# A kernel whose issue order comes from a planner: a finer model of DMA transfers, and another load order

## The chip, the cores and the metric

The kernel runs on one core of one Trainium2 chip. The metric is device time in microseconds (us) of one execution; a timed run takes about 2 us more than the span of its profile. Where two kernels are compared, the ratio is worked out from the fast runs of both in the same rounds on the same chip, so it is not quite the ratio of the medians that are quoted beside it. Runs are in the fast state but for one of e2, of e7 and of e13 and two of the four of e8; the medians are of all runs, the ratios leave the slow ones out.

Names in the profile: PE is TensorE (matmul), PEld its weight loads, DVE VectorE, ACT ScalarE, POOL GpSimd, SP the sync engine. SPq and ACTq are the queues from which SP and ACT issue DMAs.

## The reference, cut to what matters

```python
# q, k, v: (4, 8, 768, 64) float32; w_in (512, 2048), w_out (2048, 512)
scores = (q @ k.T) / 8;  keep = (pos_k < 4) | (0 <= pos_q - pos_k < 128)    # 4 sinks + window
a = softmax(where(keep, scores, -1e9)) @ v
x = a.transpose(0, 2, 1, 3).reshape(3072, 512)
h = x @ w_in
out = (h * sigmoid(1.702 * h)) @ w_out                                     # float32
```

## The kernel before

The 3072 rows are worked in 12 blocks of 256 rows (k = 0 to 11), in float16 on chip. For one block, in order:

1. `load(k)`: q, k and v (512 KB each) are loaded from the SP queue; POOL casts them.
2. `turn(k)`, from block 3 on: four transposing DMAs bring q and k into the layout that the scores need ("the q/k transposes").
3. Scores and sink scores on PE, exp on ACT, mask on DVE, then attention times v on PE and the normalization on DVE (`xb`).
4. `xturn`, from block 3 on: one transposing DMA of the normalized rows (`xT <- xb`, "the x transpose").
5. `mm1` (64 matmuls with `w_in`), tanh, `mm2` (32 matmuls with `w_out`), and the output stores.

The blocks overlap. No order is written by hand: each piece is an `Op` with a planned duration, and a list scheduler (`Plan.run`) simulates the engines at build time. The instructions are emitted in the order of the planned start times. The numbers in the plan thus reach the chip only through what the planner chooses with them: which instruction stands ahead of which in each engine's queue, and also which engine makes a cast, which buffer is taken, and how many filler matmuls (matmuls on zeros in PE's idle time at the start) are put in.

```python
HOP = {("PE", "ACT"): 60, ...}
class Plan:
    def run(self, warm=None, ...):
        ...
            free[e] = s + dur                        # the issuing engine is free again
            if isinstance(lat, tuple):               # a DMA
                dma_free = max(s + 2000, dma_free) + lat[0]
                o.end = dma_free + 300               # its data have landed
            ...
        order.sort(key=lambda x: (x[0], x[1]))       # by planned start
        return [(fn, e) for _, _, fn, e in order]

def turn(k):                                         # q/k transposes of block k, k >= 3
    ...
    casts = [o_cqk[k, p, e] for p in range(NP) for e in range(2)]
    for j in range(2):
        for i in range(2):
            def f(i=i, j=j): nc.sync.dma_start_transpose(...)
            o_t.append(op("SP", 1400, (800,), f, casts + war, prio=..., kind="turn"))

def back(k, p):                                      # attention x v, normalization
    ...
    o_t = op("SP", 2300, (1600,), lambda: nc.sync.dma_start_transpose(xT..., Xb...),
             [o_xT["n", k, q_] for q_ in range(NP)] + ..., kind="xturn")

LOADS = ["a0", "w0", "a1", "w1", "w2", "w3", "a2", "w4", "w5", "w6", "w7"]   # a: q,k,v of a block; w: weights
```

All transposes are issued from SP. The Trainium skill, "DMA: Bandwidth & Descriptors" (section "Silent corruption: two transposing streams in flight at once"), says that transposes issued from SP and from ACT can corrupt each other when both are in flight.

The softmax here doesn't subtract the row's maximum and nothing guards it: scores larger than these inputs give would overflow.

## Time and profile before

| | before |
|---|---|
| median of the first three runs | 232.47 us (230.57 to 232.59) |
| span of the profiled run | 232.3 us |
| PE busy | 94% |
| PE waits from 17 us on, plus time lost to a half-rate clock | 7.05 + 1.71 us |

The last row is summed from slices of 1 us: PE's idle part of each slice, and (1 - granted clock) times its busy part; the tail after the last matmul is left out.

The list of waits of PE in the kernel before (engine, its line, what it waited for: total us, times, longest us):

```profile
PE bank L542 <- DMA w<-qk: 2.5, 1, 2.5
PE bank L664 <- DMA xT<-xb: 1.3, 2, 0.9
...
PE bank L507 <- DMA w<-qk: 0.6, 1, 0.6
```

L542 are the scores, `w<-qk` the q/k transposes (they write into the freed weight buffers), L664 is `mm1`, L507 the sink scores. Busy time of each engine by stretch, kernel before; the columns are PE, PEld, DVE, ACT, POOL busy us (instructions), then the granted TensorE clock, the DMA share and GB/s:

```profile
60.00:64.00 4.00, 1.52 (x16) 0.74 (x15) 0.72 (x2) 1.34 (x3) 2.31 (x6) 1.00 0.74 138
64.00:68.00 4.00, 4.00 (x26) 2.05 (x25) 1.73 (x5) 1.81 (x6) 0.00 (x0) 0.57 0.68 99
...
100.00:120.00 20.00, 20.00 (x178) 13.44 (x175) 11.43 (x25) 11.26 (x22) 7.12 (x12) 1.00 0.96 205
120.00:140.00 20.00, 20.00 (x204) 13.90 (x204) 11.44 (x23) 13.65 (x28) 8.13 (x15) 1.00 0.86 169
140.00:160.00 20.00, 20.00 (x199) 13.68 (x197) 12.02 (x26) 12.30 (x24) 5.88 (x12) 1.00 0.92 163
```

There is one hole of 2.48 us at 60 to 63 us, followed by about 3.4 us at half clock (1.71 us lost); from 100 us on PE is busy all the time.

### The profile page before, as it was taken

Reading aid. Unit: us, or ns where it says so; the run is one execution under the profiler, and the core shown is the slowest. Engines: PE = TensorE matmul, PEld = TensorE weight load, DVE = VectorE, ACT = ScalarE, POOL = GpSimd, SP = SyncE. Lnnn points to the kernel's source line nnn. Section 1 sums busy time; section 2 is a strip of 40 time slices with the busy share of each in tenths; the row PEclk is TensorE's granted clock in tenths of the full one; section 3 lists DMA queues with packets and bytes.
Section 4 is the critical chain, followed back from the end, with each engine's and each line's share of the span. In section 5 each row is a group of like instructions: output and inputs, shape, how many; then the busy total and the mean of one; then the engine's idle time right before and its main releaser. Section 6 shows DMA issues by size and latency. Waiting matters only on the chain.

```text
span 232.3 us, 5342 instructions
## 1 busy us (share of the span) xinstructions
PE 218.6 (94%) x2108; PEld 150.1 (65%) x2108; DVE 127.2 (55%) x279; ACT 131.0 (56%) x258; POOL 81.1 (35%) x141
## 2 busy tenths in 40 slices
PE   8987998999599899999999999999999999999992
PEld 8764885656345576766667666766766766766640
DVE  3667977624256476466646646655645655644310
ACT  1758658243357646746656756755666676544320
POOL 6567786568704417243052262340430000000000
PEclk9999999999979999999999999999999999999999
DMA  6999999979969999698897967997974222221223
GB/s 179 335 266 395 312 324 316 324 199 252 115 97 297 157 227 219 126 294 105 200 232 130 258 128 120 261 118 150 277 121 76 48 45 48 45 55 38 45 55 80
DMA packets 74871, 41.06 MB, mean 177 GB/s; under 512 B 30688, under 2 KB 67680, under 8 KB 74848
## 3 DMA queue, kind: packets, MB, share of 16 engines
q1 hardware_dynamic: 73008, 39.73, 75.2%
q10 hardware_dynamic: 1840, 1.02, 1.5%
q8 instruction: 16, 0.26, 0.5%
q14 instruction: 7, 0.06, 0.1%
HBM read 27.36 MB, written 6.29 MB: 145 GB/s over the span
## 4 chain that ended last, share of the span: by engine, by line
PE 64%; DMA 22%; SPq 9%; POOL 2%; issue 1%; DVE 1%; ACTq 0%; ACT 0%; POOLq 0%
PE bank L692 28%; PE bank L664 27%; DMA xT<-xb 5%; DMA v<-in_v_dram 5%; DMA w<-in_moe_w_in_dram 5%; PE bank L597 4%; DMA w<-in_moe_w_out_dram 4%; SPq L446 4%; PE bank L542 3%; DMA qk<-in_k_dram 2%; SPq L371 2%; SPq L317 2%; DMA w<-qk 1%; PE bank L507 1%; POOL v L262 1%
## 5 line engine op out<-in xcount | busy, mean ns | idle before, releaser
L664 PE MATMUL bank<-xT,w_in 128*128 128x256 f16 x768 | 101.8, 273 | 1.9 <-DMA xT<-xb 1.3
L692 PE MATMUL bank<-w_out,gT 128*128 128x512 f16 x384 | 100.7, 382 | 0.7 <-POOL w_out L262 0.7
L678 DVE SCALAR_TENSOR_TENSOR gT<-th,bank 128x512 f16<-128x512 f16 x96 | 65.6, 684 | 53.2 <-ACT th L676 52.6
L664 PEld LDWEIGHTS <-w_in 128*128 128x128 f16 x768 | 72.4, 98 | 25.6 <-issue 3.7
L676 ACT ACTIVATE th<-bank 128x512 f16<-128x512 f32 x96 | 57.6, 602 | 51.7 <-PE bank L664 49.6
L560 ACT ACTIVATE at<-bank 128x512 f16<-128x512 f32 (+1 forms) x96 | 50.3, 572 | 18.6 <-PE bank L542 18.5
L692 PEld LDWEIGHTS <-gT 128*128 128x128 f16 x384 | 35.8, 98 | 24.9 <-issue 2.4
L262 POOL CAST qk<-qk 128x512 f16<-128x512 f32 x42 | 24.6, 612 | 67.1 <-DMA qk<-in_q_dram 48.4
L567 DVE TENSOR_TENSOR at<-at,bank 128x1024 f16<-128x1024 f16 (+1 forms) x48 | 30.5, 636 | 21.3 <-ACT at L560 21.1
L262 POOL CAST v<-v 64x512 f16<-64x512 f32 (+1 forms) x48 | 28.5, 593 | 10.0 <-DMA v<-in_v_dram 7.9
L597 PE MATMUL bank<-v,at 128*128 128x65 f16 x352 | 21.9, 195 | 1.0 <-DVE at L567 0.7
L597 PEld LDWEIGHTS <-at 128*128 128x128 f16 x352 | 17.8, 98 | 6.2 <-DVE at L567 2.3
L710 ACT ACTIVATE osb<-bank 128x512 f32<-128x512 f32 (+1 forms) x24 | 14.2, 590 | 13.2 <-PE bank L692 12.5
L515 ACT ACTIVATE ats<-bank 128x256 f16<-128x256 f32 x32 | 12.8, 400 | 7.2 <-PE bank L507 7.1
L615 DVE RECIPROCAL rcp<-bank 128x4 f32<-128x4 f32 x48 | 8.6, 180 | 12.6 <-PE bank L597 12.2
L617 DVE TENSOR_TENSOR xb<-bank,rcp 128x256 f16<-128x256 f32 x36 | 15.0, 420 | 0.6
L597 PE MATMUL bank<-vs,ats 128*128 128x65 f16 x128 | 15.2, 193 | 0.0
L597 PEld LDWEIGHTS <-ats 128*128 128x128 f16 x128 | 12.0, 97 | 1.8 <-issue 0.2
L542 PE MATMUL bank<-w 64*128 64x128 f16 (+1 forms) x168 | 10.3, 246 | 2.5 <-DMA w<-qk 2.5
L542 PEld LDWEIGHTS <-w 64*128 64x128 f16 x192 | 6.3, 96 | 8.0 <-issue 7.4
L758 PE MATMUL bank<-zero 128*128 128x128 f16 x109 | 10.2, 260 | 1.0 <-DVE zero L275 1.0
L262 POOL CAST w_out<-w 128x1024 f16<-128x1024 f32 x8 | 8.1, 1042 | 4.7 <-DMA w<-in_moe_w_out_dram 4.7
(40 smaller groups left out, 87.9 us busy)
## 6 DMA issues: line engine op xcount, KB each, us to landing
out_dram<-osb SPq DMA_DIRECT2D x47, 128.0 KB, 2.5
qk<-in_q_dram SPq DMA_DIRECT2D x11, 512.0 KB, 4.4
qk<-in_k_dram SPq DMA_DIRECT2D x11, 512.0 KB, 5.6
v<-in_v_dram SPq DMA_DIRECT2D x11, 512.0 KB, 7.1
w<-in_moe_w_in_dram SPq DMA_DIRECT2D x4, 1024.0 KB, 9.1
w<-in_moe_w_out_dram SPq DMA_DIRECT2D x4, 1024.0 KB, 9.6
w<-qk SPq DMA_TRANSPOSE x36, 2.9
qk<-in_q_dram SPq DMA_DIRECT2D x4, 128.0 KB, 4.0
```

The source lines that it names most:

```text
L262: {"POOL": nc.gpsimd.tensor_copy, "DVE": nc.vector.tensor_copy, "ACT": nc.scalar.copy}[e](out=out, in_=in_)
L515: o_se[k, p] = op("ACT", TB / 1.2 + 50, TB / 1.2 + 170, lambda: nc.scalar.activation(out=As, in_=f32(o_k)[:, 0:TB], func=AF.Exp, scale=scale),
L542: nc.tensor.matmul(f32(o_s, 2 * n + i)[:, c : c + w], src[d, j], Q[d].rearrange("d j s -> d (j s)")[:, q0 : q0 + w], start=True, stop=True,)
L560: nc.scalar.activation(out=A[:, i, 0:W], in_=f32(o_s, 2 * n + i)[:, 0:W], func=AF.Exp, scale=scale)
L567: nc.vector.tensor_tensor(out=A[:, :, 0:W], in0=A[:, :, 0:W], in1=mask[:, c0 : c0 + W].unsqueeze(1).to_broadcast((P, 2, W)), op=ALU.mult,)
L597: nc.tensor.matmul(avp()[:, j, i], a_, v_, start=(n == 0), stop=(n == len(mms) - 1))
L617: o_n = op("DVE", 300, 425, lambda: nc.vector.tensor_tensor(out=X, in0=avp()[:, :, :, 0:D], in1=rc.to_broadcast((P, 2, 2, D)), op=ALU.mult ...
L664: nc.tensor.matmul(f32(holder[0])[:, bass.ts(e, TB)], w_in16[:, c, bass.ts(Fi, P)], X[:, c] if k < KX else X2[:, :, c], start=(c == 0), st ...
L676: o_t = op("ACT", 477, 600, lambda first=first: nc.scalar.activation(out=th[first.places[0]], in_=f32(first), func=AF.Tanh, scale=0.851), ...
L678: o_g[k, s] = op("DVE", 565, 690, lambda first=first, s=s: nc.vector.scalar_tensor_tensor(out=g[:, 2 * s : 2 * s + 2].rearrange("p a t -> ...
L692: nc.tensor.matmul(f32(holder[0]), g[:, Fi, bass.ts(j, P)], w_out16[:, Fi], start=(Fi == 0), stop=(Fi == NF - 1),)
L710: nc.scalar.mul(O[:, c], f32(holder[0])[:, c], 0.5)
```

## The change

The planner gets a finer model of transfers: space for descriptors (the single orders of which a transfer consists) in each issuing queue's ring, eight completion slots ("lanes": a DMA waits until an earlier one on its slot has landed), a shorter delay before the first byte, a longer one until the data have landed, and new issue times of transposes. The second block's q, k and v (`a1`) are loaded ahead of all weights, and block 0's q and k are split into three DMAs each, not four; the two halves of its v change queues. No arithmetic changes. The diff is cut to what matters.

```diff
+RING, LANES = 163, 8
...
+            if isinstance(o.engs[e][1], tuple) and len(landed) >= LANES:
+                s = max(s, landed[-LANES])
...
             if isinstance(lat, tuple):
-                dma_free = max(s + 2000, dma_free) + lat[0]
-                o.end = dma_free + 300
+                ns, nd = lat
+                t = s + dur
+                while sum(n * min(1.0, (b - t) / max(b - a, 1.0)) for a, b, n in ring[e] if b > t) + nd > RING:
+                    t += 25
+                free[e] = t
+                begin = max(s + 1300, dma_free)
+                dma_free = begin + ns
+                ring[e].append((begin, dma_free, nd))
+                o.end = dma_free + 900
+                landed.append(o.end)
...
-    LOADS = ["a0", "w0", "a1", "w1", "w2", "w3", "a2", "w4", "w5", "w6", "w7"]
+    LOADS = OPT.get("LOADS") or ["a0", "a1", "w0", "w1", "w2", "w3", "a2", "w4", "w5", "w6", "w7"]
...
-                o = op("SP", 450, (1790,), f, war, prio=prio + e / 2, kind="load")
+                o = op("SP", 450, (1720, 64), f, war, prio=prio + e / 2, kind="load")
...
-                o_t.append(op("SP", 1400, (800,), f, casts + war, prio=base - 9 * h8, kind="turn"))
+                o_t.append(op("SP", 1310, (1000, 16), f, casts + war, prio=base - 9 * h8, kind="turn"))
...
-                o_t = op("SP", 2300, (1600,), lambda: nc.sync.dma_start_transpose(
+                o_t = op("SP", 1400, (1600, 16), lambda: nc.sync.dma_start_transpose(
```

In the list below X is the x transpose of blocks 3, 4, 5, ..., `t` are pieces of q/k transposes (those of block k+2 come near X of block k), L is a block's loads:

```
before: t1x4 t0x4 L X t1x4 L X t0x4 L X    t1x4    L X    t0x4    L t1   X t1x3    L t0 X   t0x3 L t1 X t1x3 X X
after:  t1x4 t0x4 L X L t1x4 X t0x4 L t1 X t1x3 L t0 X t0x3 L t1x2 t1 X t1 L t0x3 t0 X L t1x3 t1 X X X
```

In the changed kernel one or more pieces of block k+2's transposes stand ahead of the x transposes of blocks 5 to 9. In the kernel before this is so for blocks 7 to 9 only.

More of the change, by code (lines that the diff above doesn't have):

```diff
@@ L79, in run @@
         dma_free = 0.0
+        ring, landed = {e: [] for e in ENGINES}, []
         order = []
@@ L275 @@
     o_zero = op("DVE", 100, 200, lambda: nc.vector.memset(zero, 0.0), prio=NEVER, kind="const")
-    o_ident = op("ACT", 420, (300,), lambda: nc.scalar.dma_start(const, const_d.ap()), prio=NEVER + 2.6, kind="load")
+    o_ident = op("ACT", 480, (300, 8), lambda: nc.scalar.dma_start(const, const_d.ap()), prio=NEVER + 2.6, kind="load")
     def ones():
@@ L301 @@
                  [o_zero], prio=NEVER + 8, kind="const")
+    OPT = globals().get("OPT", {})
     CAST_W = ["POOL ACT"] + ["POOL"] * 7
@@ L305 @@
     CAST_V = ["POOL ACT", "POOL"] + ["POOL"] * (NK - 2)
+    CAST_W, CAST_QK, CAST_V = OPT.get("W", CAST_W), OPT.get("QK", CAST_QK), OPT.get("V", CAST_V)
     o_win, o_wout = {}, {}
@@ L316, in weights @@
             src = moe_w_out[bass.ts(j - 4, 512), :].rearrange("(c p) f -> p c f", p=P)
-        o_l = op("SP", 450, (3000,), lambda: nc.sync.dma_start(dst, src), war, prio=at, kind="w")
+        o_l = op("SP", 400, (2880, 32), lambda: nc.sync.dma_start(dst, src), war, prio=at, kind="w")
         loads.append(o_l)
@@ L327, in weights @@
             (o_win if j < 4 else o_wout)[2 * (j % 4) + n] = o
-    L = 17300.0
-    LOADS = ["a0", "w0", "a1", "w1", "w2", "w3", "a2", "w4", "w5", "w6", "w7"]
+    L = OPT.get('L',17300.0)
+    LOADS = OPT.get("LOADS") or ["a0", "a1", "w0", "w1", "w2", "w3", "a2", "w4", "w5", "w6", "w7"]
     def load_at(x):
@@ L351, in load, with f @@
         if k == 0:
-            for p in range(NP):
+            for n, (p0, p1) in enumerate(((0, 1), (1, 2), (2, 4))):
                 for e, (eng, dma, src) in enumerate((("SP", nc.sync, q), ("ACT", nc.scalar, k_ap))):
-                    def f(p=p, e=e, dma=dma, src=src):
+                    def f(p0=p0, p1=p1, e=e, dma=dma, src=src):
                         dma.dma_start(
-                            dst[:, e, 2 * p : 2 * p + 2],
-                            src[b, 2 * p : 2 * p + 2, t0 : t0 + TB].rearrange("h (p i) d -> p h i d", i=2),
-                        )
-                    lq[p, e] = op(eng, 500, (450,), f, war, prio=NEVER + 2.5 + p / 8, kind="load")
+                            dst[:, e, 2 * p0 : 2 * p1],
+                            src[b, 2 * p0 : 2 * p1, t0 : t0 + TB].rearrange("h (p i) d -> p h i d", i=2),
+                        )
+                    o = op(eng, 500, (600 * (p1 - p0), 16 * (p1 - p0)), f, war, prio=NEVER + 2.5 + n / 8, kind="load")
+                    for p in range(p0, p1):
+                        lq[p, e] = o
         else:
@@ L373, in load @@
         if k == 0:
-            o_lv = [op("ACT", 500, (900,), lv(nc.scalar, slice(0, 4)), war, prio=NEVER + 2.7, kind="load"),
-                    op("SP", 500, (900,), lv(nc.sync, slice(4, 8)), war, prio=NEVER + 2.95, kind="load")]
-            loads.append(o_lv[1])
+            o_lv = [op("SP", 500, (900, 32), lv(nc.sync, slice(0, 4)), war, prio=NEVER + 2.7, kind="load"),
+                    op("ACT", 500, (900, 32), lv(nc.scalar, slice(4, 8)), war, prio=NEVER + 2.95, kind="load")]
+            loads.extend(o_lv)
         else:
-            o_lv = [op("SP", 450, (1790,), lv(nc.sync, slice(0, 8)), war, prio=prio + 0.6, kind="load")]
+            o_lv = [op("SP", 450, (1720, 64), lv(nc.sync, slice(0, 8)), war, prio=prio + 0.6, kind="load")]
             loads.append(o_lv[0])
@@ L726, in f @@
                     )
-                o_d = op(eng, 500, (400,), f, o_c, prio=prio, kind="out")
+                o_d = op(eng, 590, (420, 4), f, o_c, prio=prio, kind="out")
                 uses("osb", oi, o_d)
```

## The prediction

> **What bounds the kernel now.** Median 232.47 us; the profiled span is 232.3 us with one state of clock (0.991). I see three stages.
> 1. 0 to about 47 us: loads. The table of engine busy time by stretch shows the DMA share at 0.94 to 1.2 in nearly every 2 us from 2 to 46 us (about 390 GB/s while weights load, 260 to 300 while q, k, v blocks load). PE, in the timeline, runs 109 filler matmuls up to 15 us; from about 21 us on it is nearly full.
> 2. 60 to 70 us: a hole. PE waits 2.48 us (60.4 to 62.9) for the four transposing DMAs of block 3, the longest PE wait in the list of waits. Its granted clock is then 0.5 from 64 to about 67.6 us (slices of 1 us), which costs another 1.75 us; then 0.57 us more for block 4's transposes. Together about 4.8 us.
> 3. 72 us to the end: PE is busy all the time in the 50 us stretches, but for 0.94 and 0.37 us before the first matmuls on transposed x. Tail after the last matmul: about 4 us.
>
> The Trainium skill, "TensorE: Matmul & The Clock Gate" (Part 1), says that the gate halves the clock after an idle window of 3.4 us; the trace agrees with the length of the penalty (3.6 us at 0.5), though here 2.5 us of idleness was enough.
>
> **What the change does.** No arithmetic is added or removed; only orders, the split of block 0's q and k loads (8 DMAs to 6), and filler matmuls (109 to 137; 52 to 56 before the first transpose, 0.105 us each cold).
> - Block 1 (1.5 MB) is loaded before w0 (1 MB). Before, w0's cast started at 13.5 us and block 1's q, k, v casts at 15.5, 17.1, 18.9 us. At the rates above block 1 comes about 3 us earlier and w0 about 5 us later; w1 to w7 land when they did, since bytes are the same. Attention 1 runs earlier while weights arrive; the first 16 mm1 matmuls (1.75 us) move behind it. By 37 us PE must again wait for w_out, so most of the lead is eaten. Net: 0.5 to 1.5 us.
> - Block 3's four transposes are issued ahead of the two output stores that kept the queue 52.57 to 55.1 us (2.53 us). Their casts ended at 52.26 us, so they can start 2.5 us earlier, but behind block 4's loads in the same rings. PE comes to these scores after 8 fewer mm1 matmuls (0.87 us), so part of the wait stays: I expect 0.5 to 1.5 us, short enough not to drop the clock. Gain 2.5 to 3.5 us.
> - Block 4's transposes now follow three pairs of stores (1.17 us each), so a wait of 0.5 to 1.5 us may stand before its sink scores. Loss up to 1 us.
> - Steady state: same matmuls, PE bound, no change.
>
> Sum: 1.0 + 3.0 - 0.5 = about 3.5 us. Predicted 228.8 us, 80% range 225.8 to 231.5. Faster by over 2%: 0.33; within 2%: 0.62; slower: 0.05.
>
> **What would show it.** Block 1's first cast near 12.5 us; PE's wait for block 3's transposes under 1.5 us and no slice below clock 0.9 near 64 us; block 4's first score at 66 to 69 us (71.5 before); PE 100% busy from 100 to 200 us as before.
>
> **What would make it wrong.** If the transposes land behind block 4's loads as late as before (62.8 us), the hole stays or grows, the clock drops again and the gain is only about 1 us. If both holes close and attention 1 fills PE from 16 us, 225 us is possible. If fillers or the weight cast in ScalarE's order hold up the first blocks, the head gets slower.

Two figures in it are off: the slices of 1 us add up to 3.4 us at half clock, not 3.6, and the changed kernel runs 123 fillers, not 137.

## More of the kernel before

The SP queue of the kernel before around the x transpose of block 5, and POOL's casts of block 7 at that time (start us, us, engine, line, operation, count, and in brackets the idle time before it):

```profile
100.67 1.14 SPq L724 DMA_DIRECT2D out_dram<-osb  x2
102.91 2.08 SPq L624 DMA_TRANSPOSE xT<-xb  x1
105.09 5.38 SPq L446 DMA_TRANSPOSE w<-qk  x4
```

```profile
100.69 1.17 POOL L262 CAST qk<-qk 128x512 f16<-128x512 f32 x2 [6.13 <-DMA qk<-in_q_dram]
102.34 1.17 POOL L262 CAST qk<-qk 128x512 f16<-128x512 f32 x2 [0.48 <-DMA qk<-in_k_dram]
```

The x transpose of block 5 goes first; the four transposes of block 7, whose casts end at 103.51 us, follow.

## The result, and the profile after

The changed kernel took 239.56 us (median of 4 runs, 239.06 to 240.17), against 231.7 us for the kernel before (4 runs); ratio 1.034, 95% interval 1.028 to 1.041. It is slower by over 3%.

The profiled spans are 237.9 and 232.3 us, 5.6 us apart. The profiled run of the kernel before took 234.08 us, more than any of its timed runs, so the two traces cover 5.6 of the 7.9 us between the medians; no trace shows the faster runs of before.

PE's waits in the changed kernel, and the same stretches as above:

```profile
PE bank L680 <- DMA xT<-xb: 7.6, 4, 3.3
PE bank L523 <- DMA w<-qk: 2.1, 1, 2.1
```

```profile
60.00:64.00 4.00, 4.00 (x49) 2.97 (x48) 3.22 (x10) 3.14 (x8) 0.00 (x0) 1.00 0.84 157
64.00:68.00 4.00, 1.93 (x16) 0.78 (x14) 2.06 (x6) 0.93 (x2) 0.00 (x0) 1.00 0.59 89
...
100.00:120.00 20.00, 16.69 (x135) 10.83 (x133) 8.99 (x20) 8.87 (x18) 6.69 (x12) 0.91 0.78 174
120.00:140.00 20.00, 20.00 (x200) 13.53 (x199) 10.66 (x22) 12.95 (x26) 7.51 (x14) 1.00 0.74 156
140.00:160.00 20.00, 17.58 (x162) 11.60 (x159) 9.99 (x20) 9.66 (x19) 6.08 (x13) 0.91 0.92 164
```

The hole at 60 to 63 us and its slow clock are gone: the wait for block 3's transposes is closed. Block 4's transposes now cost 2.07 us. And two new holes stand in the part that was full: 3.31 us near 104 us and 2.42 us near 142 us, both for an x transpose (`mm1` is L680 here), both followed by some 3.4 us at half clock. Idle time and clock loss from 17 us on are 10.64 + 3.41 us, 5.3 us more than before, which is nearly the whole difference of the spans.

Who is ahead is best read from the start of each block's first `mm1` matmul (found in the timeline by its place in the program's order):

| first `mm1` of block | before | after | after is |
|---|---|---|---|
| 4 | 92.53 us | 89.25 us | 3.3 us ahead |
| 5 | 107.88 us | 107.51 us | 0.4 us ahead: the 3.31 us hole took the lead |
| 6 | 124.10 us | 125.40 us | 1.3 us behind: the half clock, 1.7 us |
| 7 | 141.19 us | 145.07 us | 3.9 us behind: the 2.42 us hole |
| end of span | 232.3 us | 237.9 us | 5.6 us behind: another half clock, 1.7 us |

So the change won 3.3 us by block 4, close to the 3.5 us forecast for the whole, and lost 9 us between blocks 5 and 8. The SP queue of the changed kernel at the first loss, POOL's casts of block 7, and the last normalization of block 5 on DVE, which is the input of its x transpose:

```profile
94.09 0.58 SPq L379 DMA_DIRECT2D qk<-in_q_dram  x1
94.73 0.66 SPq L379 DMA_DIRECT2D qk<-in_k_dram  x1
95.43 0.66 SPq L387 DMA_DIRECT2D v<-in_v_dram  x1
96.90 3.48 SPq L740 DMA_DIRECT2D out_dram<-osb  x2
102.80 1.25 SPq L462 DMA_TRANSPOSE w<-qk  x1
104.17 1.24 SPq L640 DMA_TRANSPOSE xT<-xb  x1
105.46 3.91 SPq L462 DMA_TRANSPOSE w<-qk  x3
```

```profile
99.16 1.17 POOL L274 CAST qk<-qk 128x512 f16<-128x512 f32 x2 [7.18 <-issue]
101.61 1.17 POOL L274 CAST qk<-qk 128x512 f16<-128x512 f32 x2 [1.28 <-DMA qk<-in_k_dram]
```

```profile
98.58 0.42 DVE L633 TENSOR_TENSOR xb<-bank,rcp 128x256 f16<-128x256 f32 x1
```

```profile
107.51 1.03 PE L680 MATMUL bank<-xT,w_in 128*128 128x256 f16 x8 [3.31 <-DMA xT<-xb]
```

The input of block 5's x transpose was ready at 99.0 us and SP had ended the stores at 100.38 us. But the next entry of the queue was a piece of block 7's transposes, and its casts ended at 102.78 us. SP stood for 2.4 us, issued that piece, and only then, at 104.17 us, the transpose that PE was waiting for. The Trainium skill, "DMA: Bandwidth & Descriptors" (section "Anatomy of one DMA — SWDGE (gpsimd) path", on the fixed cost), says that DMA engines do not wait on semaphores and that any wait happens on the issuing sequencer before dispatch. The section is about DMAs issued from GpSimd, the sentence about the DMA engines; the trace of SP agrees, since SP issued nothing from 100.38 to 102.80 us.

Why did the planner choose this order? Its own times for these pieces, printed at build time (us of the plan, not of the chip), beside the trace:

| | plan | trace |
|---|---|---|
| block 7's k load: start of issue to landing | 85.92 to 91.21 (5.3) | 94.73 to 101.55 (6.8) |
| block 7's last q/k cast ends | 92.49 | 102.78 |
| first piece of block 7's transposes may start | 92.54 | 102.80 |
| input of block 5's x transpose ready | 92.71 | 99.00 |

In the plan the piece was ready 0.17 us before the other, so it went first. On the chip it was ready 3.8 us after it. The planner cannot change its mind there: it has emitted one fixed order.

At the second loss, block 7, the casts ahead were in time, but not by as much as planned: the input of the x transpose was ready at 136.94 us, and the first piece of block 9's transposes could start only at 135.39 us, 1.5 us earlier (4.1 us earlier in the plan: 121.3 and 125.45). Three pieces and two stores, 5.0 us of issuing, stood ahead of the x transpose, which went at 140.66 us:

```profile
135.39 2.54 SPq L462 DMA_TRANSPOSE w<-qk  x2
138.03 1.18 SPq L740 DMA_DIRECT2D out_dram<-osb  x2
139.25 1.30 SPq L462 DMA_TRANSPOSE w<-qk  x1
140.66 1.24 SPq L640 DMA_TRANSPOSE xT<-xb  x1
```

```profile
145.07 1.05 PE L680 MATMUL bank<-xT,w_in 128*128 128x256 f16 x8 [2.42 <-DMA xT<-xb]
```

### The profile page after: what moved, and what is told of

It is laid out like the page before. It is cut to its first block, busy times and chain, and to the rows that moved or that the text cites. A ratio compares the mean times of both kernels' runs of the same rounds, so it can differ in the third digit from the quotient of the medians.

```text
span 237.9 us, 5372 instructions
## 1 busy us (share of the span) xinstructions
PE 221.0 (93%) x2122; PEld 152.3 (64%) x2122; DVE 127.7 (54%) x278; ACT 131.3 (55%) x259; POOL 80.8 (34%) x141
## 4 chain that ended last, share of the span: by engine, by line
PE 81%; DMA 8%; ACT 3%; DVE 2%; SPq 2%; issue 1%
PE bank L680 34%; PE bank L708 31%; DMA xT<-xb 7%; PE bank L613 5%; PE bank L774 4%; PE bank L558 4%; ACT at L576 2%; SPq L462 2%; PE bank L523 1%; DMA w<-qk 1%; DVE at L583 1%; PE bank L497 1%; PE bank L652 0%; ACT ats L531 0%; DVE xn L633 0%
## 5 line engine op out<-in xcount | busy, mean ns | idle before, releaser
L680 PE MATMUL bank<-xT,w_in 128*128 128x256 f16 x768 | 100.9, 275 | 7.7 <-DMA xT<-xb 7.6
L680 PEld LDWEIGHTS <-w_in 128*128 128x128 f16 x768 | 73.5, 99 | 31.4 <-issue 8.7
L576 ACT ACTIVATE at<-bank 128x512 f16<-128x512 f32 (+1 forms) x96 | 50.1, 572 | 15.5 <-PE bank L558 15.4
L774 PE MATMUL bank<-zero 128*128 128x128 f16 x123 | 11.0, 256 | 1.0 <-DVE zero L287 1.0
L774 PEld LDWEIGHTS <-zero 128*128 128x128 f16 x123 | 9.5, 118 | 1.5 <-DVE zero L287 1.0
```

Of the source, the lines that this page charges most:

```text
L576: nc.scalar.activation(out=A[:, i, 0:W], in_=f32(o_s, 2 * n + i)[:, 0:W], func=AF.Exp, scale=scale)
L680: nc.tensor.matmul(f32(holder[0])[:, bass.ts(e, TB)], w_in16[:, c, bass.ts(Fi, P)], X[:, c] if k < KX else X2[:, :, c], start=(c == 0), st ...
L774: nc.tensor.matmul(warm_bank[:, 0:P], zero, zero, start=True, stop=True)
```

## The experiments

Thirteen runs were made, of twelve kernels (e13 is e7 once more). An *inversion* is here a piece of a later block's transposes that stands ahead of an x transpose on the SP queue. Theories: **Q**, the order on the SP queue (pieces that wait for casts, or whose issuing takes long, stand ahead of an x transpose that is ready); **H**, the new load order at the head is what costs; **D**, the x transposes land late because the DMA engines are crowded, whatever the order. All results were correct.

### e1 and e2: only the queue order changed, after the plan was made

The plan of the changed kernel is left as it is; then the pieces ahead of one x transpose (e1: block 5; e2: blocks 5 and 7) are emitted right behind it.

```diff
         order.sort(key=lambda x: (x[0], x[1]))
+        # (19 lines, told in words)
+        # for the x transposes of the blocks in XFIRST: emit the "turn" pieces found before it
+        # (back to the last load) right after it; asserted: none of their readers is emitted earlier
+        XFIRST = [5]            # e2: [5, 7]
```

> Changed kernel, with only block 5's transpose of x issued ahead of the piece of block 7's q/k transposes that stood before it on the SP queue (it waited for GpSimd's casts to 102.8 us). Theory Q (queue order): the issue of that x transpose moves from 104.2 us to about 100.4 us (end of the stores ahead), the 3.31 us PE wait at 104 to 107.5 us is gone and the clock there stays at 1.0 (it cost 1.7 us); time falls from 239.6 to about 234 to 236, and the 2.42 us hole near 142 us stays or grows. Rival H (load order at the head is what costs) and rival D (the x transposes land late because the DMA engines are crowded): no change beyond 1 us; under D the wait stays near 3 us although the issue is earlier.

> The same for block 5 and block 7 (there three pieces of block 9's transposes stood ahead). Theory Q: both holes (3.31 and 2.42 us) and both half-clock stretches (1.7 us each) go, together 9 us, so about 230 to 231.5 us, at or a little under the kernel before. Rivals H and D: 238 to 240 us.

Measured: e1 236.61 us (ratio 1.013, 1.005 to 1.021), e2 236.54 us (1.011, 1.003 to 1.019), before 232.89 us. In e1 the x transpose of block 5 is issued at 100.84 us, in place of 104.17 us:

```profile
98.68 1.97 SPq L759 DMA_DIRECT2D out_dram<-osb  x2
100.84 2.50 SPq L659 DMA_TRANSPOSE xT<-xb  x1
104.45 5.14 SPq L481 DMA_TRANSPOSE w<-qk  x4
```

```profile
106.96 1.03 PE L699 MATMUL bank<-xT,w_in 128*128 128x256 f16 x8 [0.99 <-DMA xT<-xb]
```

The 3.31 us wait became 0.99 us and the half clock behind it is gone; the hole of block 7 stayed (2.5 us). How much of that is the order? In e1's trace everything runs 1.8 us later from block 4 on (its first `mm1` is at 91.02 us, not 89.25), so count from there. In the changed kernel block 5's x transpose was issued 5.2 us after its input was ready and landed 3.3 us after that; in e1 it was issued 0.06 us after its input was ready (100.78 us), but took 6.1 us to land (106.92 us). Of the 5.1 us won in issue, 2.3 us reached PE. The columns below are as in the tables by stretch, first the changed kernel, then e1:

```profile
102.00:104.00 2.00, 2.00 (x20) 1.36 (x19) 1.79 (x5) 1.48 (x4) 1.39 (x3) 1.00 0.08 26
```

```profile
102.00:104.00 2.00, 2.00 (x19) 1.16 (x18) 0.84 (x3) 1.48 (x4) 0.75 (x2) 1.00 1.29 313
```

In the changed kernel the DMA engines ran nearly empty (share 0.08) just before the x transpose was issued, so SP's order held it and not crowding (D). In e1 it was issued behind transfers that landed up to 105.57 us, so D probably has a share in the 0.99 us that is left; no run separates that.

In e2 that one is gone too, and the next x transpose with pieces ahead of it, block 8's, shows the same picture (its input was ready at 149.98 us, it was issued at 155.22 us):

```profile
147.61 4.89 SPq L481 DMA_TRANSPOSE w<-qk  x3
152.60 1.18 SPq L759 DMA_DIRECT2D out_dram<-osb  x2
153.82 1.30 SPq L481 DMA_TRANSPOSE w<-qk  x1
155.22 1.25 SPq L659 DMA_TRANSPOSE xT<-xb  x1
```

```profile
158.41 1.03 PE L699 MATMUL bank<-xT,w_in 128*128 128x256 f16 x8 [3.22 <-DMA xT<-xb]
```

So each hole follows from its own inversion, which speaks for Q and against H and D as the cause at that place. But e1 came out 0.6 us above its forecast (234 to 236 us), and my forecast for e2 (230 to 231.5 us) was missed by 5 us, because I had counted the two holes and not the ones behind them. Mending one place let PE arrive earlier at the next.

### e3 and e4: the two parts of the change apart

e3 is the changed kernel with the old load order; e4 is the kernel before, old planner, with the new load order (one line each, the list `LOADS`).

> Changed kernel and its planner, but with the old load order (w0 ahead of block 1). Its planned SP order still has a piece of a later block's transposes ahead of the x transposes of blocks 4, 5, 6 and 7. Theory Q: still slow, 235 to 241 us, with PE waits for x transposes of over 2 us after 85 us. Rival H: back to 231 to 233 us.

> Kernel before and its old planner, with the new load order alone (block 1 ahead of w0). Its SP order has a piece ahead of the x transpose at block 5, but not at 4 and 6. Theory Q: within 2% of before, 230 to 235 us (a small hole at block 5 is possible). Rival H: 236 us or more.

Measured: e3 234.52 us (ratio 1.005, 1.000 to 1.011), e4 232.22 us (0.996, 0.991 to 1.002). e4 clears the load order alone (H falls). e3 is near the kernel before, below my forecast under Q of 235 us or more: it still has one hole of 2.5 us for an x transpose, at 138 us, but its inversions at blocks 4 to 6 cost nothing that PE's list of waits shows. At block 5, for one, the casts ended at 99.08 us and the input of the x transpose was ready at 99.49 us, so the single piece in front did not wait. So what an inversion costs depends on how long the pieces in front wait or take to issue, and on how early PE comes.

### e5: the rule given to the planner

```diff
                 o_t.append(op("SP", 1310, (1000, 16), f, casts + war, prio=base - 9 * h8, kind="turn"))
+                if k - 2 >= KX:
+                    o_t[-1].behind = o_xT[k - 2, 0][0] if isinstance(o_xT[k - 2, 0], list) else o_xT[k - 2, 0]
```

> Changed kernel, with one rule added to its planner: the transposes of block k+2 may not be planned on the SP queue before the x transpose of block k. All the pieces that stood ahead of x transposes of blocks 5 to 9 go behind; the planner adapts the other engines. Theory Q (queue order, now: every such inversion, the next one shows when one is removed): no PE wait for an x transpose over 1.6 us after 80 us, clock never below 0.9 after 80 us, and 230 to 233 us. Rival D (crowded DMA engines): 235 us or more, x transposes still awaited for 2 to 3 us.

`behind` means: not planned on its queue before that one. Measured: 231.84 us, ratio 0.996 (0.990 to 1.002), from 1.034 without the rule. Nothing of the transfer model or the load order was taken back. The test is cleaner than I had expected: built again side by side, the programs of e5 and of the changed kernel have the same instructions in the same order on PE, ACT, DVE and POOL, and only SP's differ (at 38 places). From 80 us on the longest wait for an x transpose is 1.48 us, and the clock stays full:

```profile
PE bank L525 <- DMA w<-qk: 2.1, 1, 2.1
PE bank L682 <- DMA xT<-xb: 1.8, 2, 1.5
```

This is the main evidence for Q: the order on the SP queue alone carries the whole loss. Under D, whatever the order, the waits for x transposes should have stayed at 2 to 3 us. The 1.48 us are at block 5 again, where the transpose was issued 0.12 us after its input was ready and took 6.5 us to land.

### e6: the mirror, in the kernel before

In the kernel before, the x transposes of blocks 5 and 6 are emitted behind the first piece of blocks 7 and 8.

```diff
         order.sort(key=lambda x: (x[0], x[1]))
+        # (11 lines, told in words) x transposes of blocks 5 and 6: moved behind the next "turn" piece
```

> Mirror: kernel before, with the x transposes of blocks 5 and 6 moved behind the first piece of the transposes of blocks 7 and 8, all else in the order as it was. Theory Q: x transpose of block 5 issued about 104.8 us in place of 102.9 us; PE reaches its first matmul on it at 107.9 us and it lands some 3.3 us after issue, so a wait of 0 to 1.5 us at each of the two, time up by 0.5 to 4 us. Rivals D and H: no change.

Measured: 234.15 us, ratio 1.006 (0.999 to 1.012). Block 5's x transpose was issued at 104.35 us (102.91 before) and PE waited 0.78 us for it; at block 6 there was no wait. (The larger wait in this trace, 1.76 us, is at block 4, which was not touched; the trace also has a 1.95 us wait for a weight's cast at 36 us, with 3.4 us at half clock behind it.) The sign and the size fit Q, but the interval includes no change at all and the profiled spans of both are 232.3 us, so e6 alone shows nothing. Its wait of 0.78 us does show that the same inversion is cheap where PE is not ahead: in the changed kernel PE came to block 5 three microseconds sooner.

### e9 and e10: which number of the planner made the order

e9 changes one constant of the changed planner, the landing delay of q, k and v loads; e10 puts one constant back, the planned issue time of an x transpose.

```diff
-                o.end = dma_free + 900
+                o.end = dma_free + (2600 if o.kind == "load" else 900)      # e9
```

```diff
-                o_t = op("SP", 1400, (1600, 16), lambda: nc.sync.dma_start_transpose(
+                o_t = op("SP", 2300, (1600, 16), lambda: nc.sync.dma_start_transpose(      # e10
```

> Changed kernel, with one constant of its planner changed and no rule: q, k and v loads are taken to land 2.6 us after their last byte's slot, not 0.9 us (in the changed kernel's run the k load of block 7 landed 6.9 us after its issue began, against 5.2 us in the plan). The planner then puts the x transposes of blocks 5 and 6 first by itself; a piece still stands ahead of those of blocks 7, 8, 9, as in the kernel before. Theory P (the planner's too early landings made the harmful order): 230.5 to 233.5 us, no PE wait over 1.6 us for x transposes after 80 us. If the order is not the cause: 237 us or more.

> Changed kernel, with another single constant put back: the planned issue time of an x transpose, 2.3 us in place of 1.4 us (measured: 1.24 us median). The planner then has the x transpose of block 5 first, but a piece ahead of those of blocks 6, 7, 8 and 9. Theory Q: part of the loss stays, 232.5 to 237 us, with a wait of over 2 us for an x transpose at one of blocks 6 to 9. Rival C (this constant is the whole cause): 230 to 232 us.

Measured: e9 233.01 us (ratio 0.996, 0.991 to 1.002), e10 233.72 us (0.999, 0.994 to 1.004), before 233.7 us in these rounds. Either constant alone is enough to bring the changed kernel back to the time before. In e9 waits for x transposes remain (the longest 2.0 us, at 103 us, without a slow clock, longer than I had expected); it is block 5's, with no piece ahead of it: output stores held its issue for 2.3 us and it took 4.5 us to land. In e10 a piece still stands ahead of the x transposes of blocks 6 to 9, and a wait of about 1.4 us near 156 us is the only one there. By the ratio, e10 went as rival C has it: the wait of over 2 us and the remaining loss that I had forecast did not come. Its program, too, differs from the changed kernel's on the SP queue alone (35 places). So no single number is "the" error: the order at block 5 hung on 0.17 us, and two quite different changes of the plan tip it.

### e7, e8, e11, e12, e13: towards a version that beats both

The output stores stood on the SP queue too, and SP waited 44.8 us in total for output tiles in the changed kernel. e7 keeps e5's rule and issues all stores from ACT, which makes the tiles; e8 does the same with the old planner and the new load order; e11 keeps the second and third pairs of stores on SP behind block 4's transposes; e12 keeps them on ACT, with the third and fourth pairs behind block 3's exponentials; e13 is e7 once more.

```diff
-                eng = "ACT" if last_tile and i else "SP"
+                eng = "ACT" if i or not last_tile else "SP"
...
-                o_d = op(eng, 590, (420, 4), f, o_c, prio=prio, kind="out")
+                o_d = op(eng, 590, (420, 4), f, o_c + ([o_m[3, p] for p in range(NP)] if k == 1 else []), prio=prio, kind="out")   # e12 only
```

> As e5, and all output stores are issued from ScalarE's queue, which makes their data, so that the SP queue never waits for an output tile (44.8 us of SP waits in the changed kernel). Theory Q: the waits for block 4's transposes (2.07 us near 66 us) and for block 3's x (1.55 us near 76 us) shrink, as six stores no longer stand ahead; 227 to 231 us, if ScalarE's 24 more us of issuing do not hold up tanh. If ScalarE becomes the limit: 233 us or more, with PE waits for its output.

> The old planner with the new load order, the same rule and the stores on ScalarE's queue. Theory Q: 227 to 231 us, like e7; a difference to e7 is then what the finer model is worth once the queue order is safe (I expect it within 1 us).

> Meant to beat both: as e7 (rule, and stores on ScalarE's queue), but the second and third pairs of stores stay on the SP queue behind block 4's transposes. In e7 ScalarE stood from 54.5 to 57.1 us and from 60.7 to 63.3 us in the issue of these stores, and PE waited 2.33 us for the exponentials behind them. Expected: that wait under 0.7 us, 227 to 229.5 us; if the stores' data then hold up the output tiles, as e7 (229.5 to 231).

> As e7, with the third and fourth pairs of stores placed behind block 3's exponentials in ScalarE's order. In e7 and e11 ScalarE stood 2.8 and 3.9 us in the issue of a store while block 4's transposes were still being issued from the SP queue, and PE waited 2.3 and 3.0 us for the exponentials behind it. Theory L (the store's issue waits for a completion slot that a queued transpose holds): that wait falls under 0.7 us, 227 to 229.5 us, ratio 0.975 to 0.987. If something else holds ScalarE there: a wait of 2 us or more remains near 64 us and the ratio is 0.985 or more.

> The kernel of e7 again, on the same chip and in the same rounds as e12, for a narrower interval: ratio 0.980 to 0.992; under theory L its PE wait of about 2.3 us near 64 us is there again.

| run | median us | before, same rounds | ratio (95%) |
|---|---|---|---|
| e7 | 230.17 | 232.42 | 0.988 (0.981 to 0.994) |
| e8 | 232.5, two of its four runs slow, the profiled one too | 232.42 | 0.990 (0.982 to 0.999) |
| e11 | 232.52 | 233.7 | 0.995 (0.991 to 1.000) |
| e12 | 231.0 | 232.77 | 0.994 (0.989 to 1.000) |
| e13 (= e7) | 231.25 | 232.77 | 0.993 (0.987 to 0.999) |

In e7 no wait that PE's list puts down to a transpose is longer than 0.2 us. In its place PE waited 2.33 us for masked exponentials, because ACT stood in a store's issue. ACT in e7 (the third pair of stores):

```profile
59.51 0.47 ACTq L742 DMA_DIRECT2D out_dram<-osb  x1
60.08 0.60 ACT L694 ACTIVATE th<-bank 128x512 f16<-128x512 f32 x1 [0.84 <-DVE gT L696]
62.84 0.50 ACTq L742 DMA_DIRECT2D out_dram<-osb  x1
63.44 1.08 ACT L694 ACTIVATE th<-bank 128x512 f16<-128x512 f32 x2 [2.76 <-DMA w<-qk]
```

The idle time ended with a q/k transpose that SP had issued: the list of waits of the built program has each DMA wait for the completion of an earlier one on its slot, eight slots in turn for both queues. In that list the store at 62.84 us waits for the slot of the first transpose of block 4, which landed at 62.82 us. In e12, with those stores behind the exponentials, the wait for them is gone; that would be so whatever had held the stores, so the slot rests on the list and these two times. But a wait of 1.64 us for block 3's x transpose came back in its place (issued 0.06 us after its input was ready, it took 8.2 us to land), and e12 is no faster than e13 (0.994 and 0.993): its forecast of 0.975 to 0.987 was missed. e11 missed too: its stores on SP left a wait of 3.0 us for the exponentials, where I had expected under 0.7. e8, without the finer model, is level with e7 (0.990 and 0.988): with the queue order made safe, no gain from the finer model is shown. The kernel of e7 and e13 is 0.7 to 1.2% faster than the kernel before (both intervals exclude no change), and by the ratios to the kernel before (0.988 and 0.993 against 1.034) some 4% faster than the changed one. That is under the 2% at which a kernel counts as faster than the one before; whether e12 differs from it is open.

## Why the prediction was wrong, point by point

- **Block 1 earlier, w0 later: right.** Block 1's first cast began at 13.77 us (forecast 12.5; 15.5 before), w0's on POOL at 18.25 us (13.55 before). PE reached block 3's scores at 58.64 us against 60.4 us, of which 0.87 us are the eight matmuls moved behind them: a gain of 0.9 us, inside the 0.5 to 1.5 us forecast. The first cast came 1.3 us later than forecast.
- **Block 3's transposes: right in mechanism, better than forecast.** I expected a wait of 0.5 to 1.5 us; PE went into the scores with about 0.1 us of gap, and the half clock did not come. About 4.2 us were won here (2.48 us of wait and 1.7 us of half clock).
- **Block 4's transposes: mis-sized.** Forecast wait 0.5 to 1.5 us, measured 2.07 us (0.57 before), so the loss is 1.5 us rather than "up to 1". Block 4's first scores came at 68.0 us, inside the 66 to 69 us forecast. Up to here the sum held (0.9 + 4.2 - 1.5 = 3.6 us, forecast 3.5), in part by luck: block 3 gave more than forecast and block 4 took more.
- **The step that failed: "Steady state: same matmuls, PE bound, no change."** It cost about 9 us (3.31 + 2.42 us of waits and twice 1.7 us of half clock), against the 3.3 us won. PE's being busy all the time in the kernel before did not mean that nothing else was near the limit; the x transposes of blocks 5 and 7 landed only 0.8 us before PE came to them. The change made PE earlier and issued these two later (at 104.17 and 140.66 us, before 102.91 and 137.08 us), because pieces of blocks 7 and 9 stood ahead of them. e5 gave the x transposes their place back, and the kernel was back at the time before.
- I had the new SP order in front of me before the prediction, with a piece of block 7's transposes ahead of block 5's x transpose, and did not ask when that piece's input would be ready. In the kernel before, block 7's casts ended at 103.51 us and the input of block 5's x transpose was ready at 102.84 us, so the trace of before already said which should go first.
- **The range of 225.8 to 231.5 us** had no term for a new hole in the steady part; my list of what could go wrong named the transposes of block 3, the fillers and the head only.

Left open: why the timed runs of the kernel before are up to 3.5 us faster than its profiled run, how much each piece of the finer model (rings, lanes, delays) shifts the order, and why x transposes took from 3.0 to 8.2 us from issue to landing in these traces. Moving x transposes to another queue was not tried, for the reason given with the kernel before.

## What to carry to other kernels

A planner's durations are only a way to choose an order; where two entries of one in-order queue are planned within a fraction of a microsecond of each other, ask which of them is worse to be late and fix that order by a rule, rather than let the model decide. Here a DMA queue was blocked by its head (SP for 2.4 us at 100 us), so an entry whose input may be late must not stand ahead of one that the busiest engine waits for. "PE is 100% busy" in a stretch says that its suppliers were in time, not that they have slack: before speeding up what feeds PE, measure the slack of every supplier there.

## What the Trainium skill lacked or had wrong

- "TensorE: Matmul & The Clock Gate" (Part 1) says that the clock is halved after at least one idle window of about 3.4 us. Here shorter gaps were enough at times: 2.42 us (changed kernel, 142 us), 2.11 us (e5, 66 us) and 1.95 us (e6, 36 us) were each followed by about 3.4 us at 0.5, while 2.07 us (changed kernel, 66 us) and 2.44 us (e13, 64 us) were not. The length of the slow stretch agrees with the page, and its statement that the window is free-running would explain why similar gaps end differently; that explanation is not shown by a run. In this kernel the penalty was 1.7 us each time, nearly as much as the gap.
- "DMA: Bandwidth & Descriptors" (section "Issuing engines are not separate DMA queues") says that issuing from several engines only saves the sequencer's time, which it calls usually small beside the DMA itself. In these runs the sequencer's time and order mattered: SP stood 2.4 us with a ready transpose behind a waiting one, and moving the stores to ACT took the waits for transposes from 3.9 us (e5) to 0.2 us (e7). The page does not spell out that an entry that waits holds back the ready ones behind it; it follows from the page's sentence on semaphore waits cited above.
- No page that I read says that DMAs of both queues share completion slots in this way: in e7 a store on ACT's queue was held for 2.8 us until a transpose issued from SP had completed. This follows from how the program was built (eight slots in turn), and is not shown to be a trait of the hardware.
